# One fixed task order for a fused top-k attention and gated feed-forward kernel

## The chip, the cores and the metric

The kernel runs on one core of a Trainium2 chip. The metric is the device time of one execution in microseconds; the kernel before takes 1394.75 us (median of 3 runs, 1394.62 to 1395.27). A core has five engines that each run their own instruction stream in order: TensorE (PE, with its weight loads shown as PEld), VectorE (DVE), ScalarE (ACT), GpSimd (POOL) and SyncE (SP, which here only issues DMAs). They wait for one another through semaphores.

## The reference

Eight batches of eight heads, 576 tokens, head size 64. Each query keeps its 32 best keys. The result, laid out as 4608 tokens by 512, goes through a feed-forward block with 2048 hidden columns.

```python
scores = scale * np.matmul(q, k.transpose(0, 1, 3, 2))
kth = np.partition(scores, -top_k, axis=-1)[..., -top_k:-top_k + 1]
scores = np.where(scores >= kth, scores, -1e9)
scores = scores - np.max(scores, axis=-1, keepdims=True)
attn = np.exp(scores)
attn = attn / (np.sum(attn, axis=-1, keepdims=True) + 1e-09)
x = np.matmul(attn, v)               # then (B,H,S,D) -> (B*S, H*D)
h = x @ w_in
out = (h * np.cos(h)) @ w_out
```

## The kernel before

The 4608 tokens are 36 blocks of 128. A block has 4 units, one for each pair of heads, so there are 144 units. Everything is float32. Work is cut into small tasks, each with one engine; a name such as `S.15` is the kind and the unit (or `F1.2.0`: block 2, bank 0). These are the kinds, with their lines:

- `QK`, `V` (SP, L186 to L215): loads. `st` (SP, L151): loads one of 32 weight chunks, whose words come as 64-bit halves and must be put together: `A` (L164, top half, ACT/POOL/DVE), `L` (L173, middle, ACT/POOL/DVE) and `W` (L184, sum, POOL). `Z` (L162) clears a weight tile before that.
- `S` (PE, L225): scores. One group makes those of two units, in two score tiles `sc` and, for the last 128 of the 576 columns, in the shared tile `rim`. `C1`, `C2` (ACT, L237, L243) copy them to SBUF: `C2` copies the ends out of `rim`.
- `D1` to `D4` (DVE, L276, L281, L299): four rounds of the search for the 8 largest. `D1` takes the larger of each two scores, and later rounds need the smaller ones, made by `LS` and `LB` (POOL, L257, L264) or by `LD` (DVE, L270). `S` of the next units may not overwrite `sc` until `D1` has read it.
- `M`, `E` (ACT, L315, L323): masking and exponentials. `DN` (DVE, L329, L334): sums and reciprocals; it may ride inside `D4`.
- Transposing a unit's weights: by DMA, with `SP`, `RD` (POOL, L339, L346), a write to DRAM `R` (SP, L352) and a transposing DMA `T` (SP, L356); or for some head units on PE with `TT`, `TL` (L367, L380, L383) and ACT copies `TC`, `TA`.
- `PV` (PE, L412): attention weights times values for a block, into the other half of `rim`. `X` (DVE, L425): scales it.
- `F1` (PE, L455): a quarter ("bank") of the first product, 4 for each block. `FV` (ACT, L465, L467), `FA` (POOL, L476, L479), `FS` (ACT, L483), `FG` (POOL, L487): h*cos(h). `F2` (PE, L495): a quarter of the second product. `O`, `OD` (L501, L504): result out.

PE also transposes the identity where it would wait (L743, L827, until planned time 130): these fills give nothing but activity.

The order on every engine is made when the program is built: a planner has a cost in microseconds for each task and picks, among those that could begin first, the one that is due first. A list `FIRST` overrules it: as long as its next task has all its predecessors, it is taken. In the kernel before, this list ends near unit 20 (block 2), and from there due times decide, corrected by the table `LATER`. Emission order is execution order on each engine, and a semaphore wait holds everything behind it on that engine. A task that writes `rim` or `sc` (kind "w": `S`, `PV`) and one that reads `rim` (kind "r": `C2`, `X`) are planned to exclude each other.

On PE the steady order of one block in the kernel before is S, F2, F1, F2, F1, S, F1, PV, F2, F2, F1 (in some blocks one F2 stands ahead of PV).

Of the kernel before, what the change touches and what calls it, by code (L numbers as in the profile page):

```python
# [31 lines left out]
def kernel(  # L32
# [126 lines left out]
    def clear(i, eng):  # L159

        tile_, at = (w_in[i], 0) if i < len(w_in) else (w_out, (i - len(w_in)) * NC)
        (nc.vector if eng == "DVE" else nc.gpsimd).memset(tile_[:, at : at + NC], 0.0)  # L162
# [349 lines left out]
    WDUE = lambda c: 0.5 + 0.30 * c if c < 16 else 5.2 + 0.25 * (c - 16)  # L512
    OTHER = {
        tuple(int(x) if x.isdigit() else x for x in word.split(".")[:-1]): word.split(".")[-1]
        for word in """
            A.3.DVE A.5.DVE A.1.POOL A.2.POOL A.12.POOL A.13.POOL A.19.POOL A.20.POOL A.21.POOL
            A.28.POOL A.29.POOL FA.1.1.DVE FA.35.2.DVE FA.35.1.POOL FA.35.3.POOL FG.1.1.DVE FG.35.0.DVE
            FG.35.3.POOL L.2.POOL L.14.POOL L.16.POOL L.17.POOL L.20.POOL L.21.POOL L.22.POOL L.26.POOL
            LOW.7.DVE LOW.11.POOL LOW.15.POOL T.0.PE T.1.PE T.2.PE T.3.PE T.5.PE T.6.PE T.7.PE T.9.PE
            T.12.PE  # L520
# [4 lines left out]
        for word in """  # L525
            Z.1 Z.4 QK.0 Z.3 QK.2 Z.0 Z.7 QK.1 Z.2 Z.6 st.14 S.0 st.13 st.0 Z.5 st.7 C1.0 V.4 C2.0 D1.0
            LS.0 st.15 LB.0 st.3 S.1 st.1 D2.0 st.4 st.5 A.14.ACT L.14.POOL QK.3 W.14 C1.2 D3.0 L.13.ACT
            A.13.POOL st.10 C1.1 V.6 W.13 C2.1 A.0.ACT D4.0 LS.1 C2.2 L.0.ACT A.7.ACT st.2 D1.1 W.0
# [2 lines left out]
            D1.2 st.6 A.4.ACT TL.0 V.2 TC.0.1.ACT W.4 S.3 M.1 LB.2 A.5.DVE TA.0 L.10.ACT st.12 D2.2
            st.25 A.10.ACT W.5 V.1 E.1 D3.2 W.10 C1.4 TT.1.1 L.2.POOL st.24 C1.3 V.7 A.2.POOL TT.1.0
            C2.3 D4.2 DN.1 W.2 L.9.ACT A.9.ACT C2.4 LS.3 D1.3 A.8.ACT st.20 QK.4 M.2 W.9 L.8.ACT LB.3
            D2.3 st.18 A.11.ACT st.28 L.11.ACT QK.5 W.8 E.2 D3.3 W.11 st.19 A.6.ACT L.6.ACT LS.4 st.30
            TC.1.0.ACT D4.3 DN.2 TC.1.1.ACT TT.2.1 L.12.ACT TT.2.0 W.6 TC.2.1.ACT D1.4 TC.2.0.ACT TL.2
            A.12.POOL M.3 st.23 TL.1 W.12 S.5 L.25.ACT D2.4 LB.4 st.21 TA.1 A.25.ACT L.24.ACT W.25 D3.4
            A.24.ACT TA.2 E.3 W.24 st.29 L.20.POOL st.22 C1.5 TT.3.0 D4.4 DN.3 A.20.POOL TT.3.1 C2.5
            TC.3.0.ACT W.20 TC.3.1.ACT TL.3 D1.5 C1.6 LS.5 st.16 TA.3 A.18.ACT PV.0 L.18.ACT LB.5
            L.28.ACT D2.5 M.4 W.18 D3.5 E.4 A.28.POOL st.27 W.28 L.19.ACT A.19.POOL C2.6 st.31 D4.5 DN.4
            W.19 L.30.ACT A.30.ACT D1.6 LS.6 st.17 M.5 S.7 W.30 A.23.ACT D2.6 L.23.ACT LB.6 st.26 E.5  # L540
            X.0 W.23 D3.6 L.29.ACT TT.5.1 A.22.ACT A.29.POOL TT.5.0 TC.5.1.ACT W.29 C1.7 A.16.ACT
            L.16.POOL F1.0.0 D4.6 DN.5 C2.7 A.27.ACT W.16 L.27.ACT D1.7 TC.5.0.ACT W.27 L.31.ACT M.6
            SP.4 F1.0.1 D2.7 A.31.ACT FV.0.0 W.31 LD.7 A.26.ACT D3.7 RD.4 A.17.ACT L.17.POOL F1.0.2 R.4
            C1.8 W.17 FV.0.1 L.22.POOL C2.8 D4.7 W.22 E.6 F1.0.3 D1.8 LS.8 M.7 T.4 LB.8 FV.0.2 D2.8
            L.26.POOL S.9 E.7 W.26 D3.8 FV.0.3 L.21.POOL TL.5 A.21.POOL TA.5 TT.6.0 C1.9 TT.6.1 W.21
            D4.8 DN.7 TC.6.0.ACT C2.9 TT.7.1 FA.0.1.POOL TC.6.1.ACT DN.6 D1.9 TC.7.1.ACT TL.7 M.8 TL.6
            LS.9 TA.6 C1.10 D2.9 TT.7.0 LB.9 C2.10 FA.0.0.POOL TC.7.0.ACT D3.9 TA.7 E.8 PV.1 LS.10
            FS.0.0 D4.9 DN.8 FA.0.3.POOL D1.10 M.9 FG.0.0.POOL S.11 LB.10 E.9 D2.10 F2.0.0 FA.0.2.POOL
            X.1 D3.10 C1.11 SP.8 C2.11 FS.0.1 TT.9.1 FG.0.1.POOL D4.10 DN.9 RD.8 F2.0.1 LS.11 C1.12 R.8
            D1.11 C2.12 FG.0.2.POOL TC.9.1.ACT M.10 LB.11 D2.11 F2.0.2 E.10 FG.0.3.POOL D3.11 T.8 LS.12  # L550
            F2.0.3 SP.10 D4.11 DN.10 D1.12 RD.10 M.11 R.10 LB.12 TT.9.0 S.13 O.0 D2.12 TC.9.0.ACT OD.0
            E.11 TL.9 D3.12 F1.1.0 TA.9 C1.14 SP.11 T.10 C2.14 C1.13 D4.12 DN.11 C2.13 F1.1.1 FV.1.0
            RD.11 D1.13 LS.13 R.11 M.12 LB.13 E.12 D2.13 F1.1.2 FA.1.0.POOL FV.1.1 D3.13 LS.14 T.11
            TT.12.1 FV.1.2 FA.1.1.DVE TC.12.1.ACT D4.13 DN.12 F1.1.3 FA.1.2.POOL FS.1.0 D1.14 LB.14 M.13
            S.15 FG.1.0.POOL D2.14 E.13 F2.1.0 D3.14 QK.6 C1.15 SP.13 C2.15 D4.14 DN.13 FV.1.3 PV.2
            RD.13 D1.15 LS.15 R.13 M.14 LB.15 E.14 FG.1.1.DVE FA.1.3.POOL TT.12.0 D2.15 F2.1.1
            TC.12.0.ACT D3.15 SP.14 FS.1.1 TL.12 TA.12 X.2 FG.1.2.POOL C1.16 D4.15 DN.14 T.13 F1.2.0
            C2.16 FG.1.3.POOL D1.16 LS.16 M.15 RD.14 E.15 LB.16 S.17 R.14 D2.16 D3.16 F2.1.2 QK.7 C1.17
            C2.17 QK.8 C1.18 LS.17 D4.16 DN.15 C2.18 F2.1.3 FV.2.0 SP.15 T.14 D1.17 M.16 LB.17 E.16
            D2.17 F1.2.1 RD.15 FA.2.0.POOL R.15 O.1 D3.17 OD.1 LS.18 F1.2.2 FV.2.1 D4.17 DN.16  # L560
# [9 lines left out]
        for word in """  # L570
            QK.0:28.613 V.0:7.458 QK.1:28.601 V.1:7.307 QK.2:-12.745 V.2:14.161 QK.3:-37.472 V.3:1.809
            S.1:-56.542 S.3:-29.889 C1.0:48.079 C2.0:-10.441 D1.0:-24.434 D2.0:25.404 LS.0:-4.3
            LB.0:-78.686 D3.0:-64.023 D4.0:30.321 M.0:-22.506 E.0:43.925 DN.0:26.97 SP.0:16.618
            RD.0:11.835 R.0:-39.513 T.0:27.558 C1.1:-8.025 C2.1:-10.788 D1.1:12.497 D2.1:-34.462
            LS.1:-9.267 LB.1:-33.642 D3.1:-44.162 D4.1:-15.056 M.1:21.715 E.1:15.979 DN.1:-29.484
            SP.1:-28.134 RD.1:-37.297 R.1:0.129 T.1:-23.408 C1.2:-35.466 C2.2:17.05 D1.2:10.357
            D2.2:-52.072 LS.2:12.918 LB.2:-4.829 D3.2:0.64 D4.2:-19.207 M.2:18.102 E.2:46.454
            DN.2:-58.233 SP.2:-18.37 RD.2:-23.361 R.2:17.991 T.2:29.869 C1.3:-57.306 C2.3:-33.137
            D1.3:-20.119 D2.3:53.031 LD.3:-3.892 D3.3:-35.245 D4.3:64.906 M.3:0.826 E.3:48.9
            DN.3:-38.387 SP.3:-21.246 RD.3:-5.98 R.3:-23.411 T.3:58.926 PV:-44.962 X:13.963 F1.0:-11.894  # L580
            FV.0:6.248 FA.0.POOL:35.295 FG.0.POOL:-24.268 F2.0:-0.924 F1.1:-21.145 FV.1:-21.187
            FA.1.POOL:24.198 FG.1.POOL:19.755 F2.1:5.932 F1.2:-4.255 FV.2:12.401 FA.2.POOL:-1.238
            FG.2.POOL:-46.3 F2.2:34.166 F1.3:-34.555 FV.3:-7.505 FA.3.POOL:62.363 FG.3.POOL:21.503
            F2.3:18.085 FS.0:-33.751 FS.1:28.441 O:27.149 OD:-65.33 TH.3:-1.91
# [157 lines left out]
    for _ in range(12):  # L742
        nc.tensor.transpose(mms[0][:, 0:P], ident, ident)  # L743
# [197 lines left out]
```

## Time and profile before

| | |
|---|---|
| time, median of 3 runs | 1394.75 us |
| profiled execution | 1394.94 us, of which span 1393.1 us |
| PE busy | 1364.2 us, 98% |
| DVE busy | 1277.2 us, 92% |
| ACT busy | 1143.5 us, 82% |
| POOL busy | 1141.7 us, 82% |
| mean granted TensorE clock | 0.990 |

The span runs from the first to the last instruction of the profiled execution. A timeline row gives start, duration, engine, line, operation, output <- input, form and count, and in brackets the idle time before it. PE instructions overlap, so the time that a piece of PE work occupies is read from its start to the start of the next piece. Matmuls are counted twice against the code's own: 64 in a row for the 32 of a `F1` bank. The form "64*64" or "128*64" is the part of the array that they use.

### The profile page before, as it was taken

To read this page: it belongs to the slowest core of one execution; us is meant where nothing else is said; L and a number is where in the kernel's file an instruction comes from. 1 tells how busy PE (TensorE), PEld (TensorE's weight loads), DVE (VectorE), ACT (ScalarE), POOL (GpSimd) and SP (SyncE) were. 2 spreads that over 40 slices of the span, in tenths; PEclk is the share of its full clock that TensorE was granted. 3 is DMA by queue.
4 is the path that set the end of the run, shared out by engine and by line. 5 is a ranking of instruction groups with operands and counts; after the bars stand their busy time and mean duration, and the time that the engine had idled before them with its cause. 6 is when DMAs were issued, how large, how long until landed. Compare 5 with 4: busy or idle time off the path is not lost.

```text
span 1393.1 us, 42908 instructions
## 1 busy us (share of the span) xinstructions
PE 1364.2 (98%) x17254; PEld 921.8 (66%) x17254; DVE 1277.2 (92%) x3718; ACT 1143.5 (82%) x2038; POOL 1141.7 (82%) x977
## 2 busy tenths in 40 slices
PE   8699999999999999999999999999999999999998
PEld 6475666666666666666667666666666666666674
DVE  8999999999999999999999999999999999999900
ACT  6997888888888888888888888888888888888832
POOL 9997788888888888888888888788888888888842
...
GB/s 289 347 58 122 154 170 182 153 190 184 179 170 141 177 192 171 183 168 197 146 194 160 158 205 161 184 155 203 170 166 177 145 188 165 143 159 148 160 97 16
DMA packets 413800, 234.25 MB, mean 168 GB/s; under 512 B 362912, under 2 KB 379552, under 8 KB 413600
## 3 DMA queue, kind: packets, MB, share of 16 engines
...
q8 instruction: 135, 2.21, 0.7%
q14 instruction: 65, 0.53, 0.1%
q10 hardware_dynamic: 224, 0.21, 0.1%
...
## 4 chain that ended last, share of the span: by engine, by line
PE 92%; POOL 3%; DMA 2%; DVE 1%; SPq 0%; issue 0%; ACT 0%; POOLq 0%; ACTq 0%
PE mm L495 36%; PE mm L455 35%; PE rim L412 11%; PE sc L225 8%; PE rim L225 2%; DMA big<-in_moe_w_in_dram 2%; POOL w_out L184 1%; POOL rest L264 1%; DMA v_more<-in_v_dram 1%; POOL sum L257 1%; DVE top L276 1%; POOL big L479 0%; DVE rest L281 0%; POOL w_in L184 0%; POOL w_out L171 0%
## 5 line engine op out<-in xcount | busy, mean ns | idle before, releaser
L455 PEld LDWEIGHTS mm<-xT,w_in 128*64 128x64 f32 x9216 | 509.2, 137 | 64.3 <-issue 62.1
L276 DVE MAX8 top<-rest 128x8 f32<-128x576 f32 (+1 forms) x864 | 526.2, 648 | 3.0 <-POOL rest L264 1.5
L455 PE MATMUL mm<-xT,w_in 128*64 128x128 f32 x9216 | 527.7, 273 | 1.2 <-ACT big L467 0.7
L495 PE MATMUL mm<-w_out,big 128*64 128x512 f32 x2304 | 518.0, 595 | 2.1 <-POOL big L487 2.1
L495 PEld LDWEIGHTS mm<-w_out,big 128*64 128x64 f32 x2304 | 159.5, 137 | 271.5 <-issue 263.1
L281 DVE MATCH_REPLACE8 rest<-top,rest 128x288 f32<-128x288 f32 (+1 forms) x576 | 337.1, 593 | 0.0
L339 POOL COPY halves<-s 128x2304 uint16<-128x2304 uint16 x135 | 284.3, 2106 | 8.1 <-ACT s L323 6.8
L315 ACT ACTIVATE s<-s,top 128x576 f32<-128x576 f32 x288 | 207.1, 768 | 30.3 <-DVE top L285 29.4
L323 ACT ACTIVATE s<-s,nd 128x576 f32<-128x576 f32 x288 | 221.1, 769 | 3.1
L487 POOL TENSOR_TENSOR big<-big,big 128x512 f32<-128x512 f32 x141 | 179.1, 1281 | 45.3 <-ACT big L483 45.3
L479 POOL TENSOR_TENSOR big<-big,big 128x512 f32<-128x512 f32 x142 | 181.9, 1281 | 11.8
L257 POOL TENSOR_TENSOR sum<-s 128x576 int32<-128x576 int32 x111 | 157.5, 1419 | 41.2 <-ACT s L243 40.6
L476 POOL TENSOR_SCALAR big<-big 128x512 f32<-128x512 int32 x142 | 88.7, 625 | 110.3 <-ACT big L467 109.9
L264 POOL TENSOR_TENSOR rest<-sum,high 128x576 int32<-128x576 int32 x111 | 157.4, 1418 | 21.6 <-DVE high L299 16.2
L237 ACT COPY s<-sc 128x896 f32<-128x896 f32 x144 | 126.5, 902 | 31.9 <-POOL big L476 21.1
L465 ACT ACTIVATE big<-mm 128x512 f32<-128x512 f32 x144 | 85.4, 593 | 79.8 <-PE mm L455 78.1
L225 PE MATMUL sc<-qk 64*64 64x448 f32 (+1 forms) x1120 | 139.7, 553 | 0.6 <-DVE high L299 0.6
L299 DVE TENSOR_TENSOR high<-sc,s 128x576 f32<-128x576 f32 x144 | 108.4, 753 | 27.7 <-ACT s L243 27.7
L276 DVE MAX8 top<-high 128x8 f32<-128x288 f32 x288 | 127.5, 456 | 5.0
L281 DVE MATCH_REPLACE8 rest<-top,high 128x288 f32<-128x288 f32 x288 | 125.4, 443 | 0.0
L243 ACT COPY s<-rim 64x256 f32<-64x256 f32 (+1 forms) x280 | 103.0, 368 | 3.8 <-DVE xT L433 0.8
L467 ACT ACTIVATE big<-mm,quarter 128x512 int32<-128x512 f32 x144 | 97.9, 680 | 0.0
...
## 6 DMA issues: line engine op xcount, KB each, us to landing
rows<-halves SPq DMA_DIRECT2D x135, 640.0 KB, 3.4
...
big<-in_moe_w_in_dram SPq DMA_DIRECT2D x16, 511.8 KB, 6.3
big<-in_moe_w_out_dram SPq DMA_DIRECT2D x16, 511.8 KB, 7.2
...
```

Source lines behind the costliest of these rows:

```text
L225: nc.tensor.matmul(to[r0 : r0 + rows, rim_bank(r0, j) if k0 else place(hp, j), 0 : k1 - k0], qs[at][d, q0 : q0 + rows], ks[at][d, k0:k1], ...
L257: nc.gpsimd.tensor_tensor(out=sums_[0].bitcast(I32), in0=s[:, :, 0:HS], in1=s[:, :, HS:S], op=ALU.add)
L264: nc.gpsimd.tensor_tensor(out=low, in0=sums_[0].bitcast(I32), in1=high_of(u).bitcast(I32), op=ALU.subtract)
L276: nc.vector.max(to[:, j], src[:, j])
L281: nc.vector.match_replace(rest[:, j], to[:, j], src[:, j], NEG)
L315: nc.scalar.activation(out=s[:, j], in_=s[:, j], func=AF.Prelu, bias=less[:, j, 0:1], scale=1.0, alpha=FAR)
L323: nc.scalar.activation(out=s[:, j], in_=s[:, j], func=AF.Exp, bias=nd[:, j : j + 1], scale=SCALE, accum_out=dens[u["n"] % 2][:, j, 0:1],)
L339: nc.gpsimd.tensor_copy(out=halves_[0][:, :, 0 : 2 * S], in_=s.rearrange("p (k h) -> p h k", h=2))
L455: nc.tensor.matmul(mm[r0 : r0 + D, a * P : (a + 1) * P], w_in[f // FC][:, c, (f % FC) * P + r0 : (f % FC) * P + r0 + D], xT[:, c], start=c ...
L479: nc.gpsimd.tensor_tensor(out=x, in0=g, in1=x, op=ALU.subtract)
L487: (nc.vector if eng == "DVE" else nc.gpsimd).tensor_tensor(out=g, in0=g, in1=x_of(b, k), op=ALU.mult)
L495: nc.tensor.matmul(o[r0 : r0 + D], g[:, at : at + D], w_out[:, f], start=f == 0, stop=f == NF - 1)
```

## The change

No computation is changed; other orders and other engines are chosen for the same tasks.

1. `FIRST` now names the tasks of the whole run in one fixed order. With it the steady block on PE is S, PV, F2, F2, F1, F2, S, F1, F2, F1, F1. `PV` follows a score group directly, and products of one kind more often follow each other.
2. Clearing the weight tiles (`Z`): DVE clears two of eight tiles where it cleared three, ACT clears one (with a multiplication by zero), POOL five.
3. Head units 6, 7, 9 and 12 are transposed by DMA and no longer on PE (T.0, 1, 2, 3, 5 stay on PE).
4. 17 identity transposes stand at the head of PE's stream where there were 12. The 33 fills that followed them ahead of `S.0` are gone; in the built program `S.0` is right behind the 17.
5. The smaller scores are made on DVE (`LD`) for units 3, 4, 6, 8, 9 where only unit 7 had it among the first ten, and for unit 15; `A.14` is done on DVE ahead of `D1.0`, `A.3`, `A.5`, `FA.1.1` and `FG.1.1` no longer. Weight loads come in another order (`st.14` ahead of `QK.2` and `QK.1`). `DN` rides in `D4` in 115 units where it did in 47.
6. The planner's costs are others, and it has a cost for turns between kinds of PE work.

```diff
     def clear(i, eng):
         tile_, at = (w_in[i], 0) if i < len(w_in) else (w_out, (i - len(w_in)) * NC)
-        (nc.vector if eng == "DVE" else nc.gpsimd).memset(tile_[:, at : at + NC], 0.0)
+        if eng == "ACT":
+            nc.scalar.mul(out=tile_[:, at : at + NC], in_=quarter[:, 0:1, None].to_broadcast([P, NC, CW]), mul=0.0)
+        else:
+            (nc.vector if eng == "DVE" else nc.gpsimd).memset(tile_[:, at : at + NC], 0.0)
...
+    ZDVE, ZACT = (0, 3), (1,)
...
-            LOW.7.DVE LOW.11.POOL LOW.15.POOL T.0.PE T.1.PE T.2.PE T.3.PE T.5.PE T.6.PE T.7.PE T.9.PE
-            T.12.PE
+            L.15.POOL L.17.POOL L.18.POOL L.23.POOL L.26.POOL L.27.POOL L.31.POOL LOW.3.DVE LOW.4.DVE
+            LOW.6.DVE LOW.8.DVE LOW.9.DVE LOW.11.POOL T.0.PE T.1.PE T.2.PE T.3.PE T.5.PE
...
     FIRST = [
-            Z.1 Z.4 QK.0 Z.3 QK.2 Z.0 Z.7 QK.1 Z.2 Z.6 st.14 S.0 st.13 st.0 Z.5 st.7 C1.0 V.4 C2.0 D1.0
...
-            FS.2.1 LS.20 D4.19 DN.18 F1.3.0 D1.20 FG.2.3.POOL T.17 M.19 LB.20 E.19 D2.20 S.21
-            FG.2.2.POOL
+            QK.0 Z.5 Z.3 st.14 QK.2 Z.4 Z.0 QK.1 Z.7 S.0 st.3 st.15 st.5 A.14.DVE L.14.POOL st.10 C1.0
+            V.1 W.14 C2.0 Z.1 D1.0 LS.0 st.6 st.9 LB.0 st.13 D2.0 st.7 S.1 QK.3 Z.2 D3.0 L.3.ACT A.3.ACT
...
+            D3.8 A.27.ACT S.9 A.26.ACT FV.0.3 L.27.POOL T.6 SP.7 C1.9 D4.8 DN.7 C2.9 FS.0.0 D1.9 RD.7
+            FA.0.3.POOL R.7 M.8 L.31.POOL D2.9 FG.0.0.POOL E.8 LD.9 FA.0.2.POOL F2.0.0 D3.9 T.7 C1.10
+            SP.8 C2.10 D4.9 DN.8 FS.0.1 RD.8 D1.10 LS.10 R.8 S.11 TA.5 LB.10 M.9 D2.10 PV.1 W.26 E.9
...
+            R.133 D1.135 M.134 LS.136 F2.31.1 E.134 D2.135 FA.31.2.POOL X.32 FS.31.1 LD.135 T.133 F1.32.0
...
+            FA.35.2.DVE FS.35.1 FG.35.2.POOL F2.35.1 FG.35.3.DVE F2.35.2 F2.35.3 O.35 OD.35
...
-    for _ in range(12):
+    for _ in range(17):
         nc.tensor.transpose(mms[0][:, 0:P], ident, ident)
...
+    TURN_COST = {("F", "S"): 0.10, ("S", "F"): 0.21, ("F", "P"): 0.15}
...
-        cost = pace.run(at, t.cost) if t.eng == "PE" else t.cost
+        cost = t.cost
+        if t.eng == "PE":
+            cost = pace.run(at, t.cost + TURN_COST.get((last_name, t.name[0][0]), 0.0))
+            last_name = t.name[0][0]
```

More of the change, by code (lines that the diff above doesn't have):

```diff
@@ L531 @@
[L531 to L560, printed above, removed]
@@ new lines @@
+            V.1 W.14 C2.0 Z.1 D1.0 LS.0 st.6 st.9 LB.0 st.13 D2.0 st.7 S.1 QK.3 Z.2 D3.0 L.3.ACT A.3.ACT
+            st.4 C1.1 W.3 A.15.ACT D4.0 C2.1 L.15.POOL st.0 A.5.ACT L.5.ACT W.15 C1.2 D1.1 L.10.ACT LS.1
+            st.2 C2.2 V.0 M.0 D2.1 E.0 LB.1 W.5 D3.1 A.10.POOL st.11 A.9.ACT L.6.ACT W.10 L.9.ACT D4.1
+            DN.0 A.13.ACT LS.2 st.8 A.6.ACT D1.2 L.7.POOL M.1 S.3 W.9 A.7.ACT LB.2 D2.2 st.24 L.13.ACT
+            E.1 W.6 D3.2 A.0.ACT TT.0.0 W.7 st.20 C1.3 V.3 TT.1.0 C2.3 W.13 L.4.ACT DN.1 A.4.ACT D4.2
@@ new lines @@
+            A.2.POOL TC.0.0.ACT st.30 L.2.ACT TT.0.1 L.0.POOL st.12 D1.3 V.2 TC.0.1.ACT W.0 M.2 TL.0 W.4
+            D2.3 L.11.ACT st.18 E.2 W.2 st.22 LD.3 A.11.POOL st.26 C1.4 D3.3 W.11 TC.1.0.ACT C2.4 TT.2.1
+            A.8.POOL st.17 L.30.ACT L.8.POOL TC.2.1.ACT D4.3 DN.2 L.24.ACT TT.2.0 W.8 TA.0 L.12.ACT
+            TT.1.1 D1.4 L.20.ACT Z.6 st.1 A.12.ACT V.5 A.30.ACT A.20.ACT W.12 D2.4 M.3 W.30 st.29 LD.4
+            TC.2.0.ACT W.20 A.24.ACT st.23 TL.1 D3.4 S.5 V.6 E.3 W.24 TC.1.1.ACT A.17.POOL TA.1 TT.3.0
@@ new lines @@
+            D4.4 DN.3 C1.5 st.19 TT.3.1 L.17.POOL st.21 C2.5 W.17 TC.3.1.ACT D1.5 TC.3.0.ACT TL.2 M.4
+            TL.3 LS.5 st.28 TA.3 LB.5 TA.2 D2.5 C1.6 C2.6 L.18.POOL L.1.ACT PV.0 D3.5 E.4 A.1.POOL W.1
+            L.29.ACT L.19.ACT A.29.POOL st.16 D4.5 DN.4 A.18.ACT V.4 W.29 A.22.ACT D1.6 L.22.ACT
+            A.19.POOL M.5 W.19 st.27 E.5 W.22 st.31 D2.6 W.18 A.16.ACT st.25 TT.5.0 LD.6 L.21.ACT TT.5.1
+            X.0 A.23.ACT L.23.POOL D3.6 A.21.ACT S.7 W.23 A.28.ACT TC.5.1.ACT W.21 L.28.ACT F1.0.0
@@ new lines @@
+            TC.5.0.ACT SP.4 D4.6 DN.5 C1.7 C2.7 A.25.ACT D1.7 M.6 RD.4 LS.7 R.4 F1.0.1 C1.8 LB.7 D2.7
+            L.25.ACT FV.0.0 W.28 D3.7 L.16.ACT E.6 W.25 F1.0.2 T.4 W.16 A.31.ACT D4.7 DN.6 C2.8 SP.6
+            FV.0.1 D1.8 FV.0.2 F1.0.3 RD.6 FA.0.1.POOL R.6 M.7 D2.8 E.7 L.26.POOL LD.8 TL.5 FA.0.0.POOL
+            D3.8 A.27.ACT S.9 A.26.ACT FV.0.3 L.27.POOL T.6 SP.7 C1.9 D4.8 DN.7 C2.9 FS.0.0 D1.9 RD.7
+            FA.0.3.POOL R.7 M.8 L.31.POOL D2.9 FG.0.0.POOL E.8 LD.9 FA.0.2.POOL F2.0.0 D3.9 T.7 C1.10
@@ new lines @@
+            F1.34.1 D2.143 LD.143 D3.143 T.141 F2.33.2 FV.34.1 DN.142 D4.143 RD.142 R.142 T.140
+            FA.34.0.POOL TH.143 M.143 F1.34.2 FA.34.1.POOL E.143 FG.33.3.POOL DN.143 F2.33.3 FV.34.2
+            FS.34.0 SP.143 RD.143 FG.34.0.POOL FA.34.2.POOL R.143 T.142 F1.34.3 O.33 FG.34.1.POOL
+            F2.34.0 T.143 FV.34.3 FA.34.3.POOL F2.34.1 OD.33 FS.34.1 FG.34.2.POOL PV.35 FG.34.3.POOL
+            F2.34.2 X.35 F2.34.3 O.34 OD.34 F1.35.0 F1.35.1 FV.35.0 FA.35.0.POOL F1.35.2 FV.35.1
+            FA.35.1.POOL F1.35.3 FS.35.0 FV.35.2 FG.35.0.DVE FG.35.1.POOL F2.35.0 FV.35.3 FA.35.3.DVE
@@ L576 @@
[L576 to L581, printed above, removed]
@@ L634 @@
         for i in range(len(chunks) // NC):
-            eng, cost = ("DVE", 2.2) if i < 3 else ("POOL", 1.75)
-            Task(("Z", i), eng, cost, i - 100.0, lambda i=i, eng=eng: clear(i, eng), lag=0.2)
+            eng, cost = [("DVE", 2.14), ("ACT", 2.4), ("POOL", 1.77)][0 if i in ZDVE else 1 if i in ZACT else 2]
+            Task(("Z", i), eng, cost, i - 100.0 if i < 7 else 5.0, lambda i=i, eng=eng: clear(i, eng), lag=0.2)
     for c in range(len(chunks)):
@@ L660 @@
             after += [("D1", i - 2, 0.95), ("LD", i - 2), ("C1", i - 2), ("C2", i - 2)]
-        t = Task(("S", group[0]), "PE", 1.05 * len(us), group[0] - SAHEAD, lambda us=us: scores(us), after, lag=0.25, kind="w")
+        t = Task(("S", group[0]), "PE", 0.995 * len(us), group[0] - SAHEAD, lambda us=us: scores(us), after, lag=0.25, kind="w")
         for i in group[1:]:
@@ L787, in __init__ @@
         def __init__(self):
-            self.full, self.k, self.busy = True, 0, 0.0
+            self.full, self.k, self.busy = False, 0, 0.0
         def next(self):
@@ L811 @@
     pace = Pace()
+    clock.update(PE=1.4 + pace.run(1.4, 2.0), DVE=1.3, POOL=1.2, ACT=3.0)
     shown = {}
@@ L822, in fill @@
             when, _, to = min((max(when, clock["PE"]), i, to) for when, i, to in spare)
+            if at - when <= 0.6:
+                return
             n = int((at - when - 0.5) * (0.7 if pace.at(when) else 0.4) / 0.115)
@@ L870 @@
                 shown = {}
-                for i in range(t.name[1], t.name[1] + round(t.cost / 1.05)):
+                for i in range(t.name[1], t.name[1] + round(t.cost / 0.995)):
                     shown[i % 2] = i
@@ L894 @@
             if ride:
-                clock["DVE"] += 0.15
+                clock["DVE"] += 0.08
                 r.begin, r.took, r.fin = at, 1.2, at + 1.2
```

284 lines of the change are left out of this document (254 added, 30 removed).

## The prediction

> **What bounds the kernel now.** I read the page's span and groups first, then busy time by stretch, and after that PE's timeline of one block. The columns of the stretches are length, busy time (instructions) of PE, PEld, DVE, ACT and POOL, granted clock, DMA share and GB/s.
>
> ```profile
> span 1393.1 us, 42908 instructions
> ...
> L299 DVE TENSOR_TENSOR high<-sc,s 128x576 f32<-128x576 f32 x144 | 108.4, 753 | 27.7 <-ACT s L243 27.7
> ```
>
> ```profile
> 11.10:136.55 125.45, 102.20 (x1084) 74.10 (x1084) 120.99 (x355) 111.84 (x218) 114.76 (x99) 0.89 0.66 207
> 139.53:1389.40 1249.87, 1249.31 (x16059) 835.77 (x16057) 1147.87 (x3347) 1025.58 (x1814) 1014.61 (x865) 1.00 0.64 165
> ```
>
> ```profile
> 691.76:728.21 36.45, 36.45 (x468) 24.67 (x468) 35.25 (x104) 30.97 (x57) 29.82 (x27) 1.00 0.78 181
> ```
>
> Two stages have different limits. From 139.53 on, PE is idle for 0.56 us in 1249.87, at clock 1.00: nothing but less or denser PE work shortens this stage. One block there takes 36.45 us, of which DVE works 35.25: it is close behind. Up to 136.55 the limit is DVE (120.99 of 125.45 busy), and PE has time over. PE's rows of one block give the price of each piece, from start to start:
>
> ```profile
> 688.11 3.71 PE L455 MATMUL mm<-xT,w_in 128*64 128x128 f32 x64
> 691.76 0.67 PE L412 MATMUL rim<-ring,v_tail 64*64 64x128 f32 x16
> ...
> 695.90 7.04 PE L495 MATMUL mm<-w_out,big 128*64 128x512 f32 x32
> 702.77 3.66 PE L455 MATMUL mm<-xT,w_in 128*64 128x128 f32 x64
> 706.36 0.98 PE L225 MATMUL sc<-qk 64*64 64x448 f32 x8
> 707.16 0.40 PE L225 MATMUL rim<-qk 64*64 64x128 f32 x8
> 707.38 0.93 PE L225 MATMUL sc<-qk 64*64 64x448 f32 x8
> 708.13 0.40 PE L225 MATMUL rim<-qk 64*64 64x128 f32 x8
> 708.46 3.65 PE L495 MATMUL mm<-w_out,big 128*64 128x512 f32 x16
> 711.94 3.66 PE L455 MATMUL mm<-xT,w_in 128*64 128x128 f32 x64
> 715.44 3.60 PE L495 MATMUL mm<-w_out,big 128*64 128x512 f32 x16
> 718.87 3.66 PE L455 MATMUL mm<-xT,w_in 128*64 128x128 f32 x64
> 722.46 0.98 PE L225 MATMUL sc<-qk 64*64 64x448 f32 x8
> ...
> 724.57 3.71 PE L455 MATMUL mm<-xT,w_in 128*64 128x128 f32 x64
> 728.11 3.60 PE L495 MATMUL mm<-w_out,big 128*64 128x512 f32 x16
> 731.64 0.67 PE L412 MATMUL rim<-ring,v_tail 64*64 64x128 f32 x16
> ```
>
> F1 ahead of F2 takes 3.50 us (711.94 to 715.44), F2 ahead of F1 3.43 (715.44 to 718.87), two F2 in a row 6.87 (695.90 to 702.77), that is 3.435 each. So a change between the two products costs nothing. What costs is a turn to or from the other kinds. Into scores: F1 ahead of S takes 3.59, 0.09 more. Out of scores: S's second `rim` piece takes 0.33 (708.13 to 708.46) where the first, ahead of more scores, takes 0.22 (707.16 to 707.38), and the product behind it is longer by 0.05 (3.48 for F2; F1 3.54 from 724.57 to 728.11). That makes 0.16. Into PV: F2 takes 3.53 (728.11 to 731.64) and F1 behind S 3.65 (688.11 to 691.76), 0.10 and 0.11 more. PV itself is 4.14.
>
> **The steady stage, from S.15.** Both orders have done the same work on PE when S.15 begins: 8 banks of F1, 4 of F2, PV.0 and PV.1. What follows is the same work too, apart from turns and the transposes below. From S.15 on the old order turns from a product into PV 34 times, the new one once (PV.35); each of the 65 score groups was followed by a product or a transpose, and in the new order 33 are followed by PV. Turns into scores stay. So 33 times 0.11 and 33 times 0.16 go, and 33 turns from S to PV come, which no row of before shows. Their bounds: nothing, as between the `rim` and `sc` pieces inside S, which are of the same form 64*64 as PV's first piece; or 0.27, if both turns just come back at the new seam. I take nothing, since the form at both sides of the seam is that of the nearest row: 33 x 0.27 = 8.9 us less. By the other end 0. The grouped products (F1 F1, F2 F2) are worth 0 by the rows above.
>
> The Trainium skill, TensorEngine Tiling (Array Packing), Key Properties, says that a change of tiling mode, and not of the tile alone, drains TensorE. The rows agree in that 128*64 next to 128*64 costs nothing and 128*64 next to 64*64 about 0.1; no row shows 64*64 scores ahead of 64*64 PV. By the rule this seam is free, and the sum is the 8.9; if any change of operands cost like one out of scores (0.16), it would be 3.6.
>
> **What the new order puts behind what.** C2 of the group ahead of PV excludes PV, which now follows at once: the ends of unit 4b+3 can only be copied 4.14 us after the scores end, and D1 of that unit waits for them. Behind this C2 on ACT stand M and E of unit 4b+2. Whether DVE notices:
>
> ```profile
> 719.19 0.75 DVE L299 TENSOR_TENSOR high<-sc,s 128x576 f32<-128x576 f32 x1
> ...
> 727.49 0.76 DVE L299 TENSOR_TENSOR high<-sc,s 128x576 f32<-128x576 f32 x1
> ```
>
> A unit lasts 8.30 us on DVE (719.19 to 727.49). S may begin when D1 has read the score tile (0.75); S 2.10, PV 4.14 and the copy of the ends (about as long as D1's 0.75, an estimate) make 7.75. So D1 of the next unit is ready 0.5 us ahead of DVE, if S begins at once, and X, which also waits for PV, adds DVE work there. I cost it at nothing: DVE hides it, with 36.45 - 35.25 = 1.2 us of a block as its reserve. It costs what exceeds that. More DN that ride inside D4 take from DVE, which is not the bound here: 0.
>
> **The head.** DVE sets the pace here, so its first task counts.
>
> ```profile
> 1.36 2.82 PE L743 MATMUL mm<-ident 128*128 128x128 f32 x12 [1.36 <-POOL ident masks.py:199]
> 3.97 4.89 PE L827 MATMUL mm<-ident 128*128 128x128 f32 x33
> 8.79 1.02 PE L225 MATMUL sc<-qk 64*128 64x448 f32 x4
> ```
>
> ```profile
> 1.38 0.57 SPq L201 DMA_DIRECT2D qk<-in_k_dram  x1
> ...
> 2.00 0.60 SPq L203 DMA_DIRECT2D qk<-in_q_dram  x1
> ...
> 5.63 1.76 DVE L162 MEMSET w_in<- 128x2048 f32 x1 [0.38 <-issue]
> ...
> 11.10 0.76 DVE L299 TENSOR_TENSOR high<-sc,s 128x576 f32<-128x576 f32 x1 [3.71 <-ACT s L243]
> ```
>
> ```profile
> rows<-halves SPq DMA_DIRECT2D x135, 640.0 KB, 3.4
> ...
> big<-in_moe_w_in_dram SPq DMA_DIRECT2D x16, 511.8 KB, 6.3
> ...
> ring<-rows SPq DMA_TRANSPOSE x135, 5.2
> ...
> qk<-in_k_dram SPq DMA_DIRECT2D x32, 16.0 KB, 3.7
> ```
>
> S.0 at 8.79 stood behind the 33 fills. 17 transposes at 2.82 / 12 = 0.235 end at 5.4, and the last keys, issued at 1.38 and 3.7 under way, are there at 5.1. So S.0 can begin at 5.4, and D1.0, 2.31 later as now, at 7.7. DVE's third clear (5.63 to 7.39) is gone and was not the limit. But A.14 now stands ahead of D1.0 on DVE and waits for st.14, issued at about 2.6; with 6.3 under way it lands at 8.9, and A.14, of the size of DVE's other half-wide operations (at most 0.75), ends at 9.6. D1.0 lies between 7.7 and 9.6; I take 8.7, 2.4 earlier than 11.10.
>
> ```profile
> 136.55 0.75 DVE L299 TENSOR_TENSOR high<-sc,s 128x576 f32<-128x576 f32 x1
> ```
>
> ```profile
> 139.53 0.98 PE L225 MATMUL sc<-qk 64*64 64x448 f32 x8
> ...
> 149.45 0.66 PE L367 MATMUL mm<-ident,s 128*128 128x128 f32 x4
> ...
> 153.62 0.33 PE L380 MATMUL mm<-ident,s 128*128 128x128 f32 x1
> ...
> 154.79 3.71 PE L455 MATMUL mm<-xT,w_in 128*64 128x128 f32 x64 [0.47 <-ACT ring L387]
> ```
>
> From D1.0 to D1.14 (136.55) DVE works 120.99 and idles 4.46. The change adds 4 LD (0.75 each by L299's mean, the same form) and takes A.3, A.5 and FA.1.1 out (at most 0.75 each): +0.75. The idle time may stay or go; the middle is 2.2. D1.14 then begins at 8.7 + 121.0 + 0.75 + 2.2 = 132.6, and S.15, which needs its first 0.75 us, at 133.6 instead of 139.53: 5.9 us less. With both ends (7.7 and no idle; 9.6 and 4.46) it is 2.7 to 9.0. PE has room for that: ahead of 139.53 it had idle time, a clock under 1, and the transposes of four more units. PE's transposes behind S.15 (0.66 at 149.45; 153.62 to 154.79 with its wait, 1.17) go: 1.8 us. Those four units go by DMA instead, 3.4 + 5.2 us and two tasks on POOL each. That is no PE work; it is later, but their PV stands behind later score groups. Four pairs of POOL's LS and LB leave in exchange, moved to DVE as LD. ACT's clear is twice as wide as its widest sine; I cost it at nothing because copies of four units' transposes leave ACT.
>
> **The sum.** 1394.94 (span 1393.1 plus 1.84 around it; 0.19 above the median of the runs) - 5.9 - 1.8 - 8.9 = 1378.3. The end of the run has the same work in both and PE still bounds it: 0.
>
> **Rivals.**
> 1. The seam S to PV costs both turns. For: no row shows it. Against: its form. 1394.94 - 5.9 - 1.8 = 1387.2. Chance 0.15.
> 2. The head gains nothing: F2.0.0 now stands ahead of S.11 and PV.1 on PE, so a late gate on POOL holds back DVE's next scores, where before S.11 went first. For: POOL is busy 114.76 of 125.45 there. Against: DVE has two units in hand. S.15 stays at 139.53: 1394.94 - 1.8 - 8.9 = 1384.2. Chance 0.2. Both 1 and 2: 1393.1, which can't be told from no change. Chance 0.03.
> 3. Slower: C2 behind PV makes DVE the bound of every block. It decides from 36.45 - 35.25 = 1.2 us of DVE idle time a block. If half of PV's 4.14 shows, a block is 35.25 + 2.07 = 37.3, 0.87 more, 33 times 29, less the head's 7.7: 1416. For: only 0.5 us of room. Against: DVE's reserve is refilled over the three other units. Chance 0.09.
> That the order is not what the list says is no rival: the built program has the new pattern through the last block.
>
> **How the numbers follow.** The forecast has 0.53. Its own range is 1374 to 1384 (head 2.7 to 9.0, some of the seam). About 2.8 us, 0.2%, can be told from no change. Faster: forecast, 1 and 2, 0.88; same 0.03; slower 0.09. The range goes from 1372 (all at the good end, 1375.2, and some us for turns read too small) to 1390 (head 2.7, transposes 1.8 and no turns: 1390.4).
>
> **What would show it.** After: S.0 near 5.4 and D1.0 near 8.7; S.15 near 133.6; PE idle under 1 us from there; blocks of 36.2 us, the last `rim` piece 0.22 ahead of PV's `v_tail`; DVE's waits for ACT's ends not above 1.2 us a block. Wrong: idle time on PE ahead of L225 with DVE as releaser in every block, or PV waiting for `ring`.

## The result, and the profile after

The changed kernel takes 1380.68 us (median of 4 runs, 1377.46 to 1384.57), the kernel before beside it 1394.89: a ratio of 0.9899, with a 95% interval of 0.9871 to 0.9927. The forecast was 1378.3 us, faster, within 1372 to 1390. The profiled execution took 1384.57 us (1.77 around the span) and is the longest of the four, so the ledger below is that of the slowest run; what sets the runs apart is the first question of the experiments.

The first line of the page of the kernel after:

```profile
span 1382.8 us, 42890 instructions
```

Busy time by stretch of the kernel after, with the columns of before: D1.0 to D1.14, S.15 to the last product, one block.

```profile
7.72:132.40 124.68, 99.71 (x1076) 75.57 (x1076) 121.92 (x358) 109.85 (x208) 117.79 (x104) 0.88 0.80 237
133.58:1379.08 1245.50, 1242.15 (x16050) 838.25 (x16048) 1138.90 (x3356) 1020.35 (x1814) 1014.05 (x865) 1.00 0.67 167
686.24:722.38 36.14, 36.14 (x472) 24.47 (x468) 34.93 (x106) 31.00 (x57) 30.59 (x27) 1.00 0.68 171
```

The block is 36.14 us where it was 36.45. But on the whole stage PE is now idle for 1245.50 - 1242.15 = 3.35 us, where it was 0.56.

| profiled executions | before | after | difference | predicted |
|---|---|---|---|---|
| start to S.15 | 139.53 | 133.58 | -5.95 | -5.9 |
| S.15 to the last product's end | 1249.87 | 1245.50 | -4.37 | -10.7 |
| what is left (of 1394.94 and 1384.57) | 5.54 | 5.49 | -0.05 | 0 |

The head came out as worked out; behind S.15 6.3 us are missing. PE's and DVE's rows of the head:

```profile
1.36 3.89 PE L961 MATMUL mm<-ident 128*128 128x128 f32 x17 [1.36 <-POOL ident masks.py:199]
5.18 1.11 PE L228 MATMUL sc<-qk 64*128 64x448 f32 x4
...
133.58 0.98 PE L228 MATMUL sc<-qk 64*64 64x448 f32 x8
```

```profile
7.08 0.76 DVE L172 TENSOR_REDUCE w_in<-big 128x512 f16<-128x512 bf16 x1 [1.83 <-DMA big<-in_moe_w_in_dram]
7.72 0.75 DVE L302 TENSOR_TENSOR high<-sc,s 128x576 f32<-128x576 f32 x1
...
132.35 0.75 DVE L302 TENSOR_TENSOR high<-sc,s 128x576 f32<-128x576 f32 x1
```

S.0 begins at 5.18 (forecast 5.4), A.14 does stand ahead of D1.0 and waits for its DMA, but that lands at 7.08 instead of 8.9, so D1.0 begins at its lower bound, 7.72. From there DVE works 121.92 us and idles 2.76, and S.15 follows 1.23 us behind D1.14, where it was 2.98. So in DVE's rows the 5.95 are 3.38 at D1.0, 0.82 up to D1.14 and 1.75 from there to S.15; that is where the times lie, not yet what causes them (experiment 3). The seam that no row of before showed, on PE:

```profile
713.30 7.16 PE L458 MATMUL mm<-xT,w_in 128*64 128x128 f32 x128
720.39 0.98 PE L228 MATMUL sc<-qk 64*64 64x448 f32 x8
...
722.16 0.40 PE L228 MATMUL rim<-qk 64*64 64x128 f32 x8
722.38 0.62 PE L415 MATMUL rim<-ring,v_tail 64*64 64x128 f32 x16
722.93 3.71 PE L415 MATMUL rim<-ring,v 128*64 128x128 f32 x64
726.47 7.04 PE L498 MATMUL mm<-w_out,big 128*64 128x512 f32 x32
```

The second `rim` piece takes 0.22 (722.16 to 722.38), as between two pieces of scores, and PV's first piece takes 0.55; PV as a whole is 4.09 us (722.38 to 726.47), where behind a product it took 4.14. The two F1 in a row (7.09) are 3.50 + 3.59, so putting products together gave nothing, as worked out. A block saves 0.31 instead of 0.27.

Where the missing 6.3 us went stands in PE's waits from 133 us on, and in the block from PV.3 to PV.4 (stretches, then PE's rows):

```profile
PE rim L415 <- DMA ring<-rows: 3.1, 4, 1.9
```

```profile
171.80:212.68 40.88, 38.96 (x475) 26.86 (x471) 34.04 (x101) 30.95 (x56) 31.48 (x27) 0.96 0.61 170
...
176.06:179.47 3.41, 3.41 (x36) 3.41 (x34) 0.00 (x0) 0.42 (x1) 2.25 (x2) 0.50 0.52 108
```

```profile
169.72 1.47 PE L228 MATMUL sc<-qk 64*64 64x448 f32 x7
...
175.11 0.44 PE L415 MATMUL rim<-ring,v_tail 64*64 64x128 f32 x4 [1.92 <-DMA ring<-rows]
175.48 5.38 PE L415 MATMUL rim<-ring,v 128*64 128x128 f32 x64
180.69 3.60 PE L498 MATMUL mm<-w_out,big 128*64 128x512 f32 x16
```

This block takes 40.88 us, 4.74 more than 36.14. PV.3 waits 1.92 us for the transposed weights of its last unit. Behind that wait the granted clock is 0.50 for 3.41 us, and PV's 128*64 pieces take 5.21 from start to start (175.48 to 180.69) instead of 3.54: the wait is paid nearly a second time, 1.67 more, about half of the 3.41. What remains lies in the pieces just ahead, whose rows overlap. The blocks from PV.6, PV.9 and PV.14 are longer too, 36.83, 37.30 and 36.82 by the same start to start: 0.69, 1.16 and 0.68. Together 7.3 us. The sum of the stage is then 33 x 0.31 = 10.2 less, 1.8 less for the transposes, 7.3 more: 4.7 less where 4.4 were measured.

The reason for the late weights is in SyncE's queue of the kernel after (L355 is R, which writes a unit's rows out, L359 is T, the transposing DMA that brings them into `ring`):

```profile
137.07 0.34 SPq L355 DMA_DIRECT2D rows<-halves  x1
...
143.88 7.96 SPq L355 DMA_DIRECT2D rows<-halves  x2
151.94 8.28 SPq L359 DMA_TRANSPOSE ring<-rows  x2
...
160.95 3.72 SPq L359 DMA_TRANSPOSE ring<-rows  x1
164.76 0.55 SPq L197 DMA_DIRECT2D qk<-in_q_dram  x1
...
168.12 3.37 SPq L359 DMA_TRANSPOSE ring<-rows  x1
```

R.12 was issued at 137.07, but T.12, which needs nothing else, is not issued before 151.94: SP issues in the order of the list, and there R.13, R.14 and T.13 stand ahead of it. So T.13, T.12, T.14 and four loads of QK.7 (164.76 to 168.0) are issued one behind the other, and T.15, the last that PV.3 needs, gets its turn at 168.12, 1.6 us before S.19 begins, and PV.3 goes on at 175.11, 7.0 us behind that issue. At the three other blocks writes of results (L507) stand between R of the block's last units and their T. Those are readings of a list; the experiments test them.

### The profile page after: what moved, and what is told of

It is laid out like the page before. It is cut to its first block, busy times and chain, and to the rows that moved or that the text cites. A ratio compares the mean times of both kernels' runs of the same rounds, so it can differ in the third digit from the quotient of the medians.

```text
span 1382.8 us, 42890 instructions
## 1 busy us (share of the span) xinstructions
PE 1349.4 (98%) x17176; PEld 920.4 (67%) x17176; DVE 1266.3 (92%) x3720; ACT 1133.7 (82%) x2026; POOL 1139.0 (82%) x978
## 3 DMA queue, kind: packets, MB, share of 16 engines
q1 hardware_dynamic: 424320, 236.54, 67.2%
## 4 chain that ended last, share of the span: by engine, by line
PE 85%; DVE 8%; DMA 3%; POOL 3%; issue 1%; SPq 0%; ACT 0%; POOLq 0%; ACTq 0%
PE mm L498 34%; PE mm L458 33%; PE rim L415 10%; PE sc L228 7%; DVE top L279 4%; DVE rest L284 3%; DMA ring<-rows 2%; PE rim L228 2%; DVE high L302 1%; DMA qk<-in_q_dram 1%; POOL rest L267 1%; POOL halves L342 1%; POOL sum L260 1%; DMA big<-in_moe_w_in_dram 0%; DVE rest L273 0%
## 5 line engine op out<-in xcount | busy, mean ns | idle before, releaser
L342 POOL COPY halves<-s 128x2304 uint16<-128x2304 uint16 x139 | 292.5, 2104 | 18.0 <-ACT s L326 14.4
L267 POOL TENSOR_TENSOR rest<-sum,high 128x576 int32<-128x576 int32 x106 | 149.9, 1414 | 12.2 <-DVE high L302 7.2
L260 POOL TENSOR_TENSOR sum<-s 128x576 int32<-128x576 int32 x106 | 150.3, 1418 | 7.4 <-ACT s L246 7.0
L228 PE MATMUL sc<-qk 64*64 64x448 f32 (+1 forms) x1120 | 142.7, 554 | 8.9 <-DMA qk<-in_k_dram 8.9
L479 POOL TENSOR_SCALAR big<-big 128x512 f32<-128x512 int32 x142 | 88.1, 620 | 25.5 <-ACT big L470 25.4
L349 POOL COPY halves<-rden 128x256 uint16<-128x256 uint16 x139 | 55.7, 401 | 52.6 <-DVE rden L337 51.7
```

The costliest lines, as they stand in the source:

```text
L228: nc.tensor.matmul(to[r0 : r0 + rows, rim_bank(r0, j) if k0 else place(hp, j), 0 : k1 - k0], qs[at][d, q0 : q0 + rows], ks[at][d, k0:k1], ...
L260: nc.gpsimd.tensor_tensor(out=sums_[0].bitcast(I32), in0=s[:, :, 0:HS], in1=s[:, :, HS:S], op=ALU.add)
L267: nc.gpsimd.tensor_tensor(out=low, in0=sums_[0].bitcast(I32), in1=high_of(u).bitcast(I32), op=ALU.subtract)
L342: nc.gpsimd.tensor_copy(out=halves_[0][:, :, 0 : 2 * S], in_=s.rearrange("p (k h) -> p h k", h=2))
```

## Experiments

Four groups. Each is timed beside the kernel before on the same chip; line numbers are those of the kernel after, two higher behind an added line.

**1. Are the waits for `ring` what separates the runs, and does SP's order make them?** The kernel after as it is, profiled again; then two edits of the task list, which only move DMA issues within SP's order; then both.

```diff
 # odlate: result writes behind the last T of their block
-R.27 OD.1 OD.2 OD.0 T.26 OD.4 T.27
+R.27 T.26 T.27 OD.1 OD.2 OD.0 OD.4
 # (and in the same way in the other blocks up to OD.18)
 # spfix: block 3
-R.13 ... R.14 ... T.13 ... T.12 ... R.15 ... T.14 ... QK.7 ... T.15
+T.12 ... R.13 ... T.13 ... R.14 ... T.14 ... R.15 ... QK.7 ... T.15
```

> The changed kernel itself, for its spread and for a second look at where PE waits. Theory L (late transposes): the 7.1 us between its runs (1377.46 to 1384.57) come from PV waiting for transposing DMAs, so a profile of a fast run shows less idle time on PE at L415 with ring as releaser, and S.15 at 133.6 within 0.5. Rival H (head): the spread arises ahead of S.15, from loads and clock there; then S.15 differs between profiles by as much as the times do.

> Only SP's order differs: result writes (OD) that stood between the write of a block's last unit and its transposing DMA stand behind that DMA. Theory L: the PE waits at PV.6, PV.9 and PV.14 (blocks longer by 0.69, 1.16 and 0.68) go and the one at PV.3 stays: 1 to 2.5 us less than the changed kernel in a like run. Rival: the DMAs themselves are slow, not their place; then the waits stay within 0.5 us.

> Only SP's order around block 3 differs: T.12 ahead of R.13, T.13 ahead of R.14, T.14 and R.15 ahead of the load QK.7, so that T.15 is issued about 4 us earlier. Theory L: PV.3 no longer waits (S.19 to the product behind PV.3 takes 6.1 us and not 10.97), 4.9 us less, median near 1377, and the runs lie within 2 us. Rival H: the spread stays near 7 us.

> Both edits of SP's order. Theory L: no PE wait of over 0.3 us behind S.15, 1376 to 1378 us, spread under 2 us. Rival H: as the changed kernel, 1377 to 1385.

| kernel | median (lowest to highest), us | ratio to before, interval | S.15, profiled run | PE's wait for `ring` |
|---|---|---|---|---|
| after, again | 1380.44 (1379.75 to 1381.37) | 0.9905 [0.9888, 0.9921] | 132.80 | 1.0 |
| odlate | 1377.89 (1377.63 to 1380.19) | 0.9888 [0.9873, 0.9903] | 132.84 | 0.4 |
| spfix | 1378.03 (1377.60 to 1380.13) | 0.9888 [0.9873, 0.9903] | 133.53 | 1.8 |
| both | 1376.46 (1375.62 to 1377.66) | 0.9875 [0.9860, 0.9889] | 131.84 | none |

The unchanged kernel, profiled again, waits for `ring` 1.0 us, in three places of at most 0.5, and its profiled run took 1379.75. Its four times lie within 1.62 us: the spread of 7.1 us did not come back, so this group could not test what made it. S.15 came at 132.80, earlier than theory L allowed.

With spfix the block from PV.3 takes 36.14, here and in the kernel with both edits; with the old order it took 36.37 to 40.88 in five profiled executions (after, again, odlate, head45, z3). So the order of SP's queue does make that wait, and how much it costs changes from run to run. The waits of spfix are at later blocks (37.98 from PV.6). With odlate the blocks from PV.6 and PV.14 take 36.14, but the one from PV.9 takes 36.98, with 0.4 of wait left, where the unchanged kernel had 37.30 and 37.06: the result writes do not explain PV.9, and its cause stays open. The medians fell by 2.4 to 2.6 us each; as fastest and slowest of each lie 2.5 to 2.6 us apart and their intervals overlap that of the unchanged kernel, neither gain is clear of the noise by itself; spfix's runs lie wider than the 2 us expected. With both, SP's queue of block 3 and the whole stage read:

```profile
139.04 3.38 SPq L359 DMA_TRANSPOSE ring<-rows  x1
...
145.92 2.79 SPq L359 DMA_TRANSPOSE ring<-rows  x1
...
153.83 2.54 SPq L359 DMA_TRANSPOSE ring<-rows  x1
...
161.46 3.66 SPq L359 DMA_TRANSPOSE ring<-rows  x1
```

```profile
131.84:1370.00 1238.16, 1238.14 (x16050) 835.23 (x16048) 1139.04 (x3356) 1021.24 (x1814) 1015.35 (x865) 1.00 0.67 168
```

T.15 is issued at 161.46, 6.7 us earlier than in the profiled run of after, and PE is idle for 0.02 us in 1238.16. That is 7.34 less than after's 1245.50, where the ledger put 7.3 on those waits, and 11.71 less than before's 1249.87, where the prediction had 10.7. The other part is the head: S.15 lies between 131.84 and 133.99 in nine profiled executions of the same head (the kernel after twice, and seven kernels that differ from it only behind S.15). The slowest of the four runs with both edits (1377.66) is below the fastest of the unchanged kernel beside them (1379.75), though not below the fastest of its first four (1377.46). By medians this version is 4.0 us faster than the kernel after and 17.6 than the kernel before (1394.1 beside them); its 2.04 us between fastest and slowest just miss the expected 2. That a run's length goes with its `ring` waits is seen in two profiled runs (1384.57 with 3.1, 1379.75 with 1.0, of which 0.78 is the head); for the three other first runs it is inferred, and why a DMA of one and the same order lands late in some runs stays open.

**2. Is the seam free because of its form?** One matmul more between S and PV, in 32 blocks: of the products' form 128*64, or of S's and PV's 64*64. Its result is written over by PV.

```diff
 def values(...):
+    if us[0]["n"] >= 3 * NP and us[0]["n"] < 35 * NP:
+        # seam128
+        nc.tensor.matmul(room[0][0:D, 0:P], w_in[0][:, 0, 0:D], ident, start=True, stop=True)
+        # seam64, in its place
+        nc.tensor.matmul(room[0][0:D, 0:P], w_in[0][0:D, 0, 0:D], ident[0:D], start=True, stop=True)
```

> The changed kernel with one more matmul of the products' form (128 rows of the array, a 128x64 tile of w_in times the identity, 128 wide) between the scores and PV in blocks 3 to 34; PV overwrites its result. Theory T (turns of form): the seam S to PV is free because both sides are 64*64, so a single 128*64 piece there brings both turns back: a block goes from 36.14 us to about 36.14 + 0.27 + 0.055 (a 32nd of F1's 3.5, halved for its half width) = 36.45 to 36.5. Rival N (a turn is just a change of operands): one piece more costs 0.05 to 0.1: 36.2.

> The control: the same extra piece at the same place, but from 64 rows (form 64*64). Theory T: only the piece itself, 36.2 us a block. Rival N: the same 36.2; rival O (any extra piece breaks the run): 36.4 or more, as in the kernel with the 128*64 piece.

PE's rows with the 128*64 piece, then with the 64*64 piece (the dots stand for rows that overlap, among them the second record of the 64*64 piece):

```profile
687.02 0.40 PE L228 MATMUL rim<-qk 64*64 64x128 f32 x8
687.35 0.43 PE L398 MATMUL rim<-ident,w_in 128*64 128x128 f32 x2
687.71 0.67 PE L417 MATMUL rim<-ring,v_tail 64*64 64x128 f32 x16
...
691.85 7.04 PE L500 MATMUL mm<-w_out,big 128*64 128x512 f32 x32
```

```profile
719.94 0.40 PE L228 MATMUL rim<-qk 64*64 64x128 f32 x8
720.16 0.27 PE L398 MATMUL rim<-ident,w_in 64*64 64x128 f32 x1
...
724.45 7.04 PE L500 MATMUL mm<-w_out,big 128*64 128x512 f32 x32
```

With 128*64 the `rim` piece ahead takes 0.33 again, and from it to the product 4.83 us pass (687.02 to 691.85). With 64*64 it takes 0.22 and 4.51 pass. The kernel after has 4.31 (722.16 to 726.47). So the piece costs 0.52 in the one form and 0.20 in the other; the 0.32 between them is the two turns. Blocks take 36.66 and 36.34, each 0.1 to 0.2 more than theory T had: the piece itself is dearer than the bare estimate, and the difference between the two is what T said. Rivals N and O fall. Whole runs: 1394.53 (ratio 1.0002 [0.9991, 1.0012]) against 1385.05 (0.9933 [0.9913, 0.9953]), 9.5 us apart for 32 x 0.32 = 10.2. A seam that cost both turns would have eaten nearly the whole of the steady stage's gain. The Trainium skill, TensorEngine Tiling (Array Packing), Key Properties, says that a change of tiling mode drains TensorE and a change of tile alone does not; these two runs agree, and put 0.32 us on leaving a mode and coming back.

**3. What is the head's gain made of?** Three pieces apart: the 28 transposes that no longer stand ahead of S.0, given back; the old kernel with an early S.0; and the clears alone.

```diff
 # head45, on the kernel after
-    for _ in range(17):
+    for _ in range(45):
 # b17, on the kernel before
-    for _ in range(12):
+    for _ in range(17):
...
-        if at < FILL and spare:
+        if 8.0 < at < FILL and spare:
 # z3, on the kernel after
-    ZDVE, ZACT = (0, 3), (1,)
+    ZDVE, ZACT = (0, 1, 3), ()
```

> The changed kernel with 45 identity transposes at the head of PE's stream for its 17, as many as stood ahead of S.0 before. Theory D (DVE paces the head, and its first task decides): S.0 at about 8.8, D1.0 at 11.1 to 11.4 for 7.72, and S.15 later by 3.4 less the 1.0 and 0.4 that DVE now waits in its first units: 135.6 to 137 for 133.6, and the time 2 to 3.4 us longer. Rival A (absorbed): the head waits elsewhere (loads of QK.3, decoded weights), S.15 moves under 0.7 us.

> The kernel before with only the head of PE's stream changed: 17 transposes, no fills planned ahead of time 8, so S.0 stands right behind them; fewer fills follow in the first 70 us; all other orders are the same. Theory D: D1.0 near 7.7 for 11.10, S.15 2 to 3.4 us earlier than 139.53 and the time as much shorter, 1391 to 1393. Rival A: the old order's later waits (1.88 at 127.58 on DVE, the gate at 108.6 on PE) take it back, under 0.7 us.

> The changed kernel with the clears as before in number: DVE clears three tiles at its start, ACT none. Theory (clears hidden): the third clear (1.76 and 0.38 ahead of it) falls into DVE's wait of 1.8 to 3.1 us for the first weight chunk, so D1.0 is later by 0.3 at most, S.15 lies between 131.8 and 134, and the time is that of the changed kernel (1380.4 to 1380.7) within 1.5. Rival: ACT's clear was worth its 2 us, or D1.0 moves by the whole clear; then S.15 at 135 or later, or 1.5 us earlier.

| kernel | S.0 | D1.0 | S.15 | time, us | ratio to before, interval |
|---|---|---|---|---|---|
| before | 8.79 | 11.10 | 139.53 | 1394.89 | |
| b17 | 4.91 | 7.31 | 137.99 | 1393.33 | 0.9992 [0.9983, 1.0002] |
| after | 5.18 | 7.72 | 133.58 | 1380.68 | 0.9899 [0.9871, 0.9927] |
| z3 | 5.17 | 9.73 | 133.60 | 1379.40 | 0.9893 [0.9877, 0.9910] |
| head45 | 9.20 | 11.51 | 135.71 | 1383.16 | 0.9922 [0.9907, 0.9936] |

In the new order a D1.0 that begins 3.8 us later costs 2.1 us at S.15, and 2.4 us of the time by the ratios of again and head45 (0.9905 and 0.9922, whose intervals overlap). In the old order a D1.0 that begins 3.8 us earlier brings S.15 forward by 1.5 only, less than the 2 to 3.4 of theory D and more than the 0.7 of rival A; b17 has fewer fills as well, and a granted clock of 0.85 there for 0.89. DVE's waits in b17:

```profile
DVE top L276 <- POOL rest L264: 4.0, 5, 1.7
DVE high L299 <- ACT s L243: 1.7, 1, 1.7
```

```profile
7.31:135.01 127.70, 100.93 (x1035) 71.69 (x1037) 121.13 (x356) 111.39 (x218) 117.24 (x101) 0.85 0.68 211
```

It waits 4.0 us for POOL's LB (L264), and idles 6.57 us between D1.0 and D1.14 where before idled 4.46. But DVE is not what S.15 waits for at the end: in all three kernels S.15 begins when the F1 ahead of it on PE ends. PE's rows of F2.0.1, from which the same three F2, four F1 and one score group lead to S.15, in before, b17 and after, and the stretch of before with the low clock:

```profile
108.60 12.22 PE L495 MATMUL mm<-w_out,big 128*64 128x512 f32 x48 [2.13 <-POOL big L487]
...
107.19 12.08 PE L495 MATMUL mm<-w_out,big 128*64 128x512 f32 x48 [2.26 <-POOL big L487]
...
105.46 3.60 PE L498 MATMUL mm<-w_out,big 128*64 128x512 f32 x16
```

```profile
108.67:112.08 3.41, 3.41 (x10) 0.97 (x12) 3.38 (x14) 3.35 (x8) 3.41 (x4) 0.50 0.49 188
```

In before and b17 F2.0.1 waits for POOL's FG (L487), and from there to S.15 it is 30.93 and 30.80 us; in after it follows PV.1 without a wait and it is 28.12 (in the kernel with both edits of SP's order it waits 1.01 us for POOL, from 103.67 on it is 28.17, and the clock stays at 1.00). So of the 5.95, 3.14 lie in when F2.0.1 can begin and 2.81 behind it. There the transposes of unit 9 on PE are gone (1.1 us). And the three F2 take 12.14 in before (108.60 to 120.74), 1.8 more than in its steady blocks, with the granted clock at 0.50 for 3.41 us; in after it is 1.00 from 105.46 to 133.58. b17's 1.5 are what POOL's gate moved: 1.41 from 108.60 to 107.19.

The early S.0 is worth about 1.5 us in the old order and 2.1 in the new, as far as single profiles can tell: by the nine executions of the unchanged head, in which S.15 moves by itself over 2.15 us, the 2.1 may be 1.7 to 3.9. The rest of the head's 5.95 comes from the order and what it moves off POOL, which no run separates. D1.0 at 9.73 in z3 was expected at most 0.3 later than 7.72, but it lies between 7.45 and 9.67 in those nine too, and z3 moves neither S.15 nor the time by what can be told: the clears, on whichever engine, are worth nothing.

**4. How far is the slower rival?** X, the copy behind PV on DVE, is done twice or three times over from block 3 on (0.69 us of DVE work each).

```diff
-... lambda us=us: take_values(us), [("PV", b), ...
+... lambda us=us, b=b: [take_values(us) for _ in range(2 if b >= 3 else 1)], [("PV", b), ...
 # x3: 3 in place of 2
```

> The changed kernel with X (DVE, 0.69 a block) done twice from block 3 on: how much room DVE has behind PE, the point from which the slower rival would decide. DVE works 34.93 to 35.63 of 36.14 us. Theory R (room of 0.5 to 1.2 a block): blocks stay within 0.3 us of 36.14. Rival S (the score ends behind PV leave no room): blocks grow by 0.6 or more, 20 us in all.

> X three times, 1.38 us more DVE work a block: 36.3 to 37.0. Theory R: DVE is now the bound, blocks of 36.4 to 37, PE waits for DVE ahead of L228, 10 to 28 us longer. If blocks stay at 36.14, DVE's room is larger than its busy time shows; if they grow by the full 1.38, there was none.

Twice over gives 1387.19 us (0.9947 [0.9932, 0.9963]), three times 1412.55 (1.0133 [1.0113, 1.0153]). PV's first pieces follow each other in the kernel with X twice:

```profile
796.79 0.62 PE L415 MATMUL rim<-ring,v_tail 64*64 64x128 f32 x16
...
832.93 0.62 PE L415 MATMUL rim<-ring,v_tail 64*64 64x128 f32 x16
```

and PE waits, from 200 to 1260 us, in the kernel with X three times:

```profile
PE mm L498 <- POOL big L490: 6.7, 10, 0.9
PE mm L458 <- ACT big L470: 4.5, 11, 1.2
PE mm L458 <- DVE xT L428: 4.0, 7, 1.9
PE rim L415 <- DMA ring<-rows: 2.9, 3, 1.5
```

With 0.69 more this block and some like it still take 36.14; others grow (20 of the 31 from PV.3 to PV.34 stay within 0.3 us), and 6 to 7 of the 22.8 us of added work show. Some of that is waits for `ring` (2.7 us from 200 to 1260, 1.2 in after's profiled run), some for X itself (1.1); where the rest stands was not followed up, so x2 is mixed between the two theories. With 1.38 more DVE would have 36.3 us of work in 36.14, and PE begins to wait for POOL, ACT and DVE ahead of F1 and F2, not ahead of L228 as expected; most blocks take 36.6 to 37.3. Another 25.4 us, more than the 22.8 added, show, so that the kernel is 32 us slower than after, over the 10 to 28 expected; 3.55 of them lie in the block from PV.3 of the profiled run, 40.72 here, where PV waits for `ring` as in after. So the bound changes hands between the two: of the 1.2 us that DVE idles in a block, about 0.5 were used in x2 at no cost.

## Why the prediction was right

Its sign and place and the sizes of its terms held; one term was sized at nothing and was 7.3 us in the profiled run, and the reason given for the head's term was wrong.

- **The steady stage, from S.15.** "I take nothing, since the form at both sides of the seam is that of the nearest row" held: 0.22 ahead of PV, and experiment 2 shows that it is the form. 33 x 0.27 was 33 x 0.31, since PV's first piece is also 0.05 shorter behind scores. Rival 1 falls.
- **What the new order puts behind what.** C2 behind PV cost PE nothing, as taken, though the text named the unit wrongly (the scores ahead of PV.b are those of unit 4b+7, and the M and E behind it are of 4b+6; the argument is the same). DVE's waits in the kernel after, from 200 to 1260 us, have changed their names:

```profile
DVE high L302 <- ACT s L246: 17.0, 17, 2.2
DVE xT L428 <- ACT s L246: 11.0, 9, 1.9
...
DVE xT L436 <- ACT s L246: 2.4, 2, 1.2
```

  30.4 us behind C2 in 29.3 blocks, 1.04 a block, below the 1.2 that the text allowed. Rival 3's mechanism is there; by x2 and x3 it decides only with 0.7 to 1.4 us more DVE work in a block. That x3's 1412.55 lies near the rival's 1416 says nothing for its size: there added work shows, not half of PV.
- **The head.** S.15 at 133.58 for 133.6, out of D1.0 1.0 us earlier than taken, idle time 0.6 longer and work 0.2 longer. Rival 2 (S.15 stays) falls. That the number fits to 0.02 is luck: in nine executions of the same head S.15 lies between 131.84 and 133.99. What was wrong is "DVE sets the pace here, so its first task counts". DVE was busy for 120.99 of 125.45 us, but in before POOL's gate at 108.60 and PE's stream behind it set S.15, by b17 the first task alone brings a quarter of the gain, and in the nine executions a D1.0 at 7.45 goes with S.15 at 133.53 and one at 9.67 with 133.55.
- **PE's transposes behind S.15.** 1.8 us, not tested by itself; with the waits gone (both edits of SP's order) the stage is 11.71 us shorter, for 33 x 0.31 + 1.8 = 12.0.
- **The step that failed** is the sentence on the four units that now go by DMA: "That is no PE work; it is later, but their PV stands behind later score groups." That cover was named and not measured. Their T's were not followed through SP's queue, where they stand behind R's, four loads and each other: with 3 to 4 us for each of them T.15 is issued 1.6 us before S.19, and lands 7.0 later, far behind the end of S.19. It cost 4.7 us at PV.3 in that run; result writes in SP's queue, which the prediction does not weigh at all, cost 1.4 at PV.6 and PV.14, and 1.16 at PV.9 are not explained. In four other profiled executions with that order PV.3's block cost 0.2 to 2.3 us more than 36.14. The prediction's own sign of error, "PV waiting for `ring`", is what appeared. Without this term the profiled run gives 1377.3 us, 1.0 from the forecast.
